# Masking a segment's attention on VectorE with a minimum instead of a TensorE product, with an instruction order made for it

## The chip, the cores and the metric

One core of one Trainium2 chip runs the whole program in one launch. The metric is device time in microseconds (us); lower is better. The kernel before takes 815.55 us, the median of three runs (813.28 to 816.82).

## The reference

Two attentions over the same 2048 rows are mixed by a gate. The change touches only the first, the recurrent one. It goes through 64 segments of 32 rows. Each segment is preceded by 8 memory rows, which are the first 8 output rows of the segment before, so the segments form a chain.

```python
mask = (idx[:, None] < M) | (idx[:, None] >= idx[None, :])   # M = 8, L = 40
for s in range(n_seg):                                       # 64 segments
    h = concatenate([mem, xs]);  q, k, v = h @ Wq, h @ Wk, h @ Wv     # 32 heads of 128
    scores = where(mask, q @ k.T * scale, -1e9)
    o = softmax(scores) @ v @ Wo
    mem = o[:, :M];  outs.append(o[:, M:])
...
return g * a + (1 - g) * b        # b: the second attention, g: the gate
```

A masked score has to count as nothing in the softmax: its exponential must be zero.

## The kernel before, in words

**Parts.** `p_seg` issues one segment. It works in two passes, r = 0 and r = 1, of 16 heads each. The second attention (`p_bproj`, `p_piece`, `p_bout` and others, in units), the projections of the rows that become memory keys (`p_rest`) and the output product of later rows (`p_orest`) do not depend on the chain; they are work that can stand anywhere between.

**One segment.** K, Q and V projections (`wproj`, line 1422) in groups of four products that run side by side on four 32-column strips of the array; each result is copied out of PSUM by `copy` (lines 1000 to 1004, ops `kev`, `qev`, `vev`), which may run on ACT or on DVE. K and Q are transposed on DVE (line 1497, `ktp`, `qtp`). Then for each pass:

- `H` (lines 1504 to 1506): a product of two constant tables, `neg` (a diagonal of -1e9) and `hide` (ones where the mask hides), into 160 of the 224 columns of a PSUM bank. It writes -1e9 at the masked places and 0 elsewhere, and it opens the accumulation (`start=True`).
- `S` (lines 1508 to 1520): 16 score products of 40 columns and 4 of 64, added on top of it.
- `exp` (line 1521): ACT takes the exponential of the 224 columns into `PT` (bf16).
- `U` (line 1536): a product with ones gives the sums; `ln` and `rc` (lines 1540, 1542) on ACT make the reciprocal in f32.
- `nrm` (line 1544) and `nrr` (line 1546): `PT` is multiplied by the reciprocal, in two parts; `nrm` on DVE, `nrr` on DVE or GpSimd.
- `PV`, `PW` (lines 1577, 1586): the products with V; `OTev` copies their result out of PSUM.

The output product follows (`wo`, line 1314), then the transpose of the memory rows (`turn`, `swap`, `hm`, lines 1332 to 1337), which the next segment's projections need.

**Order.** Each of the five engines (PE for TensorE, DVE for VectorE, ACT for ScalarE, POOL for GpSimd, SP for SyncE) runs its instructions in a fixed order. `sequences` unpacks it from the string `ORDER`: for each engine a list of operations, which also says which engine does a copy that may run on either. `schedule` walks these lists; `waits` sets the semaphore waits. The order is so written out beforehand, and nothing is rearranged while the kernel runs.

**Tables.** `p_init` fills `neg` and `hide` (lines 844 to 854) with GpSimd selects at the start; the last of them ends at 37.1 us of the profile, and the first `S` starts at 49.81 us.

Of the kernel before, what the change touches and what calls it, by code (L numbers as in the profile page):

```python
# [8 lines left out]
ALU = mybir.AluOpType  # L9
# [10 lines left out]
    "jybi^^oj}%>U%zo>Jb8OZ<N}L1(=#JDDoS_`pkgh2B0%=U>r|~rbo`cqusO2TW~0a<WCe1=<RUh>xlYGAT@awnt*sMpDAF5er(SIgaCr*VEC!Gp!1GiZ{)5^AJm?7j_+?@1XVC66"  # L20
    "fK}v0dtnjOMt8&ES#TM#+-5CV24f)gF^mT=dd2_h7_tMPi`R}>Q*C+|IKc{F8M+b*CahBw{|@l86F&Jw<gJA$VEhbw5jb2flMdk9=>lxN@wK9KSIXHo05@sWTy_w|B0V@xG|X$k!"
    "5Qc(z>l4d0gO{L*8zySK|+AI=Yc|?i|A>-rv~5b&x$60G`~bF5g;`*UeUgp8#$P~WuO<H3;HrU6qp@?poi!G*1ZFJdo>Z@TR5FXf;4NkN4_;Q_>=tEN6g`@fLb1bpaQZOiBXA>+V"
    "H_fUo0j7tZRV`qWIE%l9QVe4i}WBen=dJJ$-3R$`vD)ECd(}i!6v}wbKMbU|KIybFj0I<yVs21`WWjcz74CIxX<zN6}V_>`=sknfI7Lom-iDQqlY4j3tj35S_u#NIL8@#(|@(^gD"
    "q0MO1`W<fvwgK|q|<WpWYQIAZErNVb+NA!hN)%6Z)m)oCLd#K2<P`G#<>Spirme1+>R!DTrEufjoS2e3LBmW(FSix)!Cv_)X{<k$nW+{BAwE4V<Gi@XNJ6qu-J|I%D~`W1pX(dr6"
    "(Zsdy$M1J#|UcaIjK_A87OP!BGmm~3{MiDW2`b1JS#zG4zYL8z&jn!$w&VgMtAR!PCfvr_vXm#I&D5^58Xr!WX?sD?;Wsu1EGvETU^t@Rm^QJ;WnomV`C2^nywC;mQ$Yfy?Ur|D_"
    "+x^7LIRr4fPb(%|7#Kycye@;J*805BKVblW2D^Y*GHwNd0uQboqwdro;&<wLP(!K-hDODb5;6!@=<%CuNDROMkMxyQ!@7G&;`g2uwoqyYIK2&-U4g}V{#iBP3SzT(=$yDIx0r};d"
    "Nfrr`}5L`NyOOQqQPFs*-F9YE_D=Av!#v~1t^1;Pt@?xMDN{1dK?MP(&QfgfDlfp4L48({ACl!_Z={bdSQl?kBP9gHeF!YDiZ}!fSaJ`F@)>OoG{{7l9QCr;5++xqT}nYJ(f%ef~"
    "c~)u+~#VO0>bU0*1m<2xW-kOk04bH`epzFFYc_HvHD-Ka11iv=>z?H<I=tQX?Qxb~61n`atq8hKl#IxN?r?i*2q4HEG5LAY^gk%flVv+w|Ack1N&eV+-P*$I%~$fqC(V=2F6+_tK"
    "`$8cX!18sAl7csb{#;Jk*=Paxt!Za1~P%cZhXN^zu1U15uA4^8D0gNtMmY~^4ON{QNWB&IM|jnZ6*Xhn-kCz4tQhr7rk=C+VQPuR<@C=B(ynW-%49~@;K9!UNyT@S$JF#tytozt5"
    "C5q%x@h_(LpPy`V@*Acw6w7TY-iq_!{C<tnj^Sg(%r<~diL6o##{=@EL37^jN263L+F9ox%n6xg^Gt&DDu=FUTEBz%LVBu$V;StF#Po6I_Sl#@!P^<e$H^}ZKKyE(N>>^7aeuavs"  # L30
    "k{{#SP{$7ig0u5Y#H#>}Wt<&{zDiRhT?0mtAHBEmPeKPL;WPxrHfu(gCf6ag`T(LL?1@J_fS6ROGaBXcH@L-8_<H^ipOtaX;r-0nFvbWeghvU(DST1;KExcXR$dh9w3HG@%d90<&"
    "ZW<b$c$)3=>3m_l&*Y%8{2^}?JvWB^OX~U;fkSdIUfR$4m;v2B`Bx%y#9>54MH3xB7MT$<H0T`m}T6&coXW6Tz;aqV#X!tpSC9S7t)}gBN}W{riGy>zgB*<TzR7uy-}OUuQyyO)-"
    "siOn$h@AL#ivGJ0EhjT1YoyYvW@MFLY>wp|);&Ib8AT;<D}gmu1TFWeRi2Xv>GoU=hpKt%IM&zyT+LjSMg{%J4pXZF;3H(_mrLFQqV+Mk!eItZb1NzWE}MK`K&_YyvM`A%AvKzYV"
    "6M0H<G6fTl+~AFZw|9zwo$KKdS=2?!i51O%%Fm0IS_mN~K|<SP-X20y3A9NgotFGgo9z#&ED)b^)HyWPWZdZABn)#r-7Kv>_;>|+c47YjIdg`vPoNGMcK=SH8l(t6$@=uwE7Cp>8"
    "J4G5f9fY3Gsdp_1c|2}SxF2o#+IoO!z`7&Dd$OV5rg4fas^_$65>v`>`tO75lLm)1OSd4-&iXHX_h^bH?qYv@SS-tpTj8@=i{0!Fx@dx;B>^y*$&Ibf2aaey?M-8ZvZ+2K906G;w"
    "WHuyZ#$|TBj5~wi3Yz~Vw*NjLKy;YPcpls)v}Wj_Jww``O8;rn?AhSbTfj}M4%p7)QNd<#1yT{P@4!jC%?t&m@28UsI&1?}pF;uNPRSB&F4OJ+^+iK~Symw&j*0|(Ke%>FY#=)BN"
    "0spfp&%?Kz=B6z9)ysf+03461+@^^-o}?i&M^U}c-C+77cFah+fy~TfT9r3H41Qh_k%GH?u0wY8qIIZc3Da0hh!jwt)LdMEzr%qwFd=0Yf$sPLpEI?83~L)1Ja1Ir4Am7O(Z5i7H"
    "sQrz;oYifr9W2n9Nw<l2@YM>RO+vTNqYiL!3<xQL)MTck{vq0&;jvo<Gh^0@8rGT41v2z;L1?*n+3d2;pr7mOweE(dIlIws*&e8XG)n-JF5!io%L><BK7Hv&ktcHjy~mb#d?~jV!"
    "hHj}G5V!QGw)64V9AOABTQzYPI(_@{P9>#MSPW`ymLx8jZ+ez)#j6d+sV=8A(zM$#eqPWZlF9-{?1D%y77{uvWcu*Wk2=1nIHIxroS<Q3gq^AiCitVL6|%S*}&loDNz?@|#Ovrg7"
    "tVs-B{y-BQ})dBi8M82qy(AlnBfoa~TlvstPHxaIbt8p>sJ>DE0b{9e41Ft?THB#-==UG!__3IXK+mmE1QP(Vx{pH-D1WKNm@Fcc2U4-G+QC{ppooCOXH7RU|H$SZ$i`v6)H=-7b"  # L40
    "VYu9TE#oa2e;Z&jsaRW&V{)EovUA||DA8f|LP&=Ln{Y%?&x_<KQD;2W0SBf{m_LaM<h6(5pzs2C2JQ12AqAhbglp-*#);na7n|lyhXr4N4HEHLgWwPD#SSD!HVDR{8{Tu6y*US{T"
    "kwLx);kMarJ>-i{{Z3k#8<PtesK_jfMBE~8$sYcJX(AOU-e^=7McSr$ZHXiS};|I!wb9Pdqj^{>_L5m!wW)1Ls6Lb%H0O&)dMxW-~+*eaNMm3PL2ezgRlUCx~tOTlSM@YAZOAy(+"
    "z^dU-Z??&t7;^!!dagxF)QSuheG>mt@P{{&6k&yP1Anj1uhzysfLXqOsecGwI$Kd#-IvuRHeD@OQnTYhdUyFp@WD)?z{RsFYnxlhNo;lcTNY6C1fJ96$HrHx0|rXq`8t&3>?OYX?"
    "<)v4CH<205=bz9qa^@ie%`w2z&>@rdipAA1>}Y<sNaEnKu|7!KOjkIQ_`aOA`+2z);0%UvJ+8~U&==D!`yqx>Z^gP?-f8^WGLRxBJYiwogJsIWS%SPX(jZ_m)f`L?y(R5c1SxjAF"
    "em3A((TYd)g<DKgO4K}3}ggy+(tB<TAIIyr_ivBEgIMqG7`|tZV8~Nw9D~(7yxX?66;Pox<=z@QIw_#p%1sPj_sQLbL4t`I7jDfJ_Z8&ptNO=pV37awgBQ*N`wG}1~GOjj$hb(@x"
    "$L$wMgZv5_=6w(3`p8ws<7k`RxA?wD+K|&itkvnWA-iuO*&o67enCHF?^!q*%58Z1OtOy7fU|ejn+1Dczju7PY33VEZbgYEJY~*<8jquiU0IN@um83IuqEc;fV9~lbWf`VqK&)Wm"
    "@~|T_g<pj2L%-x!C1<pcE^eLHa#6l!5o)a|8f)IZe0_I*B$SjT>DXlfrGOT6Un`zj+c|WkZq92lVI-X?FktNt3M_87S^#sd~n-hT=Dtxk;_RShz%LNchAa`N5NyA-ii47OK#CbjE"
# [1600 lines left out]
```

## Time and profile before

| | us |
|---|---|
| median of the three runs | 815.55 |
| lowest and highest | 813.28, 816.82 |
| the profiled execution | 813.89 |
| its span, first to last instruction | 811.9 |
| TensorE busy, of the span | 788.2 (97%) |
| VectorE busy | 643.7 (79%) |
| ScalarE busy | 523.1 (64%) |
| GpSimd busy | 257.8 (32%) |

The span is what the rows of the trace cover; 2.0 us of the profiled time lie around it. "PE" in the rows is TensorE's matmul side and "PEld" its weight loads, which overlap it. A matmul's row gives its length, while the next one may start before it ends, so what a matmul costs TensorE is read from the starts, or from the chain of waits, where overlap is taken out. `x4` beside a row counts instructions. The clock that TensorE was granted is 1.00 of full speed over the whole span.

### The profile page before, as it was taken

The page shows a single profiled execution, that of the slowest core. Times are in us where ns is not written, and L with a number is a line of the kernel's source. Part 1 is how long each engine was busy: PE and PEld are TensorE (multiplying, and loading weights), DVE is VectorE, ACT ScalarE, POOL GpSimd, SP SyncE. Part 2 cuts the span into 40 slices and gives each one's busy share as a digit, 9 for nine tenths or more (in the row PEclk, how much of TensorE's full clock was granted, in tenths as well). Part 3 has the DMA queues.
Part 4 walks back from the last instruction along what each step waited for, and adds up shares of the span by engine and source line. Part 5 has one row for each costly group of instructions (what it writes and reads, how often), then busy time and mean ns, then how long its engine had stood idle before and what let it go on. Part 6 is the DMA issues. An engine that isn't in the chain of part 4 may idle for free.

```text
span 811.9 us, 51762 instructions
## 1 busy us (share of the span) xinstructions
PE 788.2 (97%) x23598; PEld 501.2 (62%) x23607; DVE 643.7 (79%) x1681; ACT 523.1 (64%) x1198; POOL 257.8 (32%) x564
## 2 busy tenths in 40 slices
PE   9899999999999999999999999999999999999987
PEld 4456666666666666666666665656766665666655
DVE  4878887788889787787787887786877898787886
ACT  4666656776666656767667666577666656766662
POOL 4542221233223332422422322333323223432440
PEclk9999999999999999999999999999999999999999
DMA  8983202121200111121011111100111010010001
GB/s 327 417 256 63 47 16 45 36 52 27 48 25 21 46 27 40 33 46 34 21 33 48 38 25 42 30 24 20 40 48 31 21 31 21 16 25 22 22 21 37
DMA packets 71696, 45.14 MB, mean 56 GB/s; under 512 B 50046, under 2 KB 69942, under 8 KB 69942
## 3 DMA queue, kind: packets, MB, share of 16 engines
q1 hardware_dynamic: 70422, 40.92, 17.8%
q8 instruction: 185, 3.03, 1.6%
q10 hardware_dynamic: 1056, 0.92, 0.4%
q14 instruction: 33, 0.27, 0.1%
HBM read 30.33 MB, written 8.87 MB: 48 GB/s over the span
## 4 chain that ended last, share of the span: by engine, by line
PE 84%; DVE 8%; DMA 3%; ACT 2%; issue 2%; SPq 1%; POOL 1%; DVEq 0%; POOLq 0%; ACTq 0%
PE pb L1422 46%; PE pb L1314 18%; PE pb L1029 6%; PE pb L1146 3%; PE pb L1187 2%; PE pb L1577 2%; DMA st<-in_gate_w_dram 2%; PE pb L1512 2%; PE pb L1536 1%; PE pb L1031 1%; DVE V_sb L1002 1%; PE pb L1586 1%; DVE st L1002 1%; PE pb L1235 1%; DVE QT_sb L1497 1%
## 5 line engine op out<-in xcount | busy, mean ns | idle before, releaser
L1164 ACT ACTIVATE PTB<-pb 128x640 bf16<-128x640 f32 x240 | 158.5, 705 | 41.0 <-PE pb L1146 29.8
L1002 ACT ACTIVATE st<-pb 128x512 bf16<-128x512 f32 (+2 forms) x232 | 112.9, 499 | 104.3 <-PE pb L1422 76.1
L1422 PE MATMUL pb<-Wv_sb,hT 128*32 128x512 bf16 x2048 | 152.5, 380 | 0.0
L1422 PE MATMUL pb<-Wq_sb,hT 128*32 128x256 bf16 (+1 forms) x3072 | 139.2, 308 | 0.3
L1314 PE MATMUL pb<-Wo_sb,OT_sb 128*32 128x256 bf16 x4096 | 130.8, 273 | 2.2 <-issue 1.8
L1422 PE MATMUL pb<-Wk_sb,hT 128*32 128x512 bf16 x2048 | 131.1, 379 | 1.2 <-issue 0.9
L1314 PEld LDWEIGHTS pb<-Wo_sb,OT_sb 128*32 128x32 bf16 x4096 | 102.3, 96 | 12.6 <-issue 2.3
L1170 POOL TENSOR_SCALAR_AFFINE_SELECT PTB<-PTB 128x512 bf16<-128x512 bf16 x120 | 77.7, 648 | 90.2 <-ACT PTB L1164 82.2
L1422 PEld LDWEIGHTS pb<-Wq_sb,hT 128*32 128x32 bf16 x3072 | 79.7, 97 | 42.4 <-DVE hT L1337 4.4
L1546 POOL TENSOR_TENSOR PT_sb<-PT_sb,rc_sb 128x64 bf16<-128x64 bf16 x81 | 28.9, 356 | 188.9 <-ACT rc_sb L1542 174.9
L1422 PEld LDWEIGHTS pb<-Wk_sb,hT 128*32 128x32 bf16 x2048 | 53.2, 97 | 49.6 <-DVE hT L1337 2.3
L1002 DVE CAST st<-pb 128x512 bf16<-128x512 f32 (+1 forms) x123 | 67.2, 549 | 15.4 <-PE pb L1422 12.7
L1002 ACT ACTIVATE OT_sb<-pb 128x320 bf16<-128x320 f32 (+1 forms) x139 | 57.4, 429 | 32.2 <-PE pb L1586 31.3
L1002 DVE CAST OT_sb<-pb 128x320 bf16<-128x320 f32 (+2 forms) x121 | 56.5, 475 | 18.5 <-PE pb L1586 17.6
L1002 DVE CAST V_sb<-pb 128x512 bf16<-128x512 f32 x90 | 61.5, 684 | 8.8 <-PE pb L1422 7.9
L1497 DVE STREAM_TRANSPOSE QT_sb<-st 128x128 f32<-128x128 f32 (+1 forms) x192 | 61.8, 335 | 8.3 <-ACT st L1002 6.4
L1540 ACT ACTIVATE rc_sb<-pb 128x160 f32<-128x160 f32 x128 | 38.9, 304 | 42.7 <-PE pb L1536 36.2
L1332 DVE STREAM_TRANSPOSE pb<-pb 128x256 f32<-128x256 f32 x63 | 29.3, 465 | 40.7 <-PE pb L1314 40.4
L1521 ACT ACTIVATE PT_sb<-pb 128x224 bf16<-128x224 f32 x128 | 45.5, 356 | 23.0 <-PE pb L1516 19.1
L1422 PEld LDWEIGHTS pb<-Wv_sb,hT 128*32 128x32 bf16 x2048 | 48.0, 97 | 20.0 <-ACT st L1002 0.7
L1497 DVE STREAM_TRANSPOSE KT_sb<-st 128x256 f32<-128x256 f32 x128 | 54.6, 427 | 7.0 <-ACT st L1002 5.5
L1544 DVE TENSOR_TENSOR PT_sb<-PT_sb,rc_sb 128x160 bf16<-128x160 bf16 x128 | 45.2, 353 | 8.9 <-ACT rc_sb L1542 7.3
(200 smaller groups left out, 1449.4 us busy)
## 6 DMA issues: line engine op xcount, KB each, us to landing
Wv_sb<-in_A_Wv_dram SPq DMA_DIRECT2D x4, 1024.0 KB, 11.2
Wk_sb<-in_A_Wk_dram SPq DMA_DIRECT2D x4, 1024.0 KB, 19.3
Wq_sb<-in_A_Wq_dram SPq DMA_DIRECT2D x4, 1024.0 KB, 26.6
Wo_sb<-in_A_Wo_dram SPq DMA_DIRECT2D x4, 1024.0 KB, 22.2
rest_v<-stg SPq DMA_DIRECT2D x112, 32.0 KB
rem_v<-rest_v SPq DMA_DIRECT2D x28, 128.0 KB, 2.5
a_rows<-ao SPq DMA_DIRECT2D x63, 32.0 KB
stg<-a_rows SPq DMA_DIRECT2D x15, 128.0 KB
```

The source lines that it names most:

```text
L1002: self.P.op(("act", "dve"), (lambda a: a.activation(dst, src(), ACT.Copy), lambda d: d.tensor_copy(dst, src())), reads=reads, writes=write ...
L1029: ins = pe.matmul(out[32 * c:32 * c + 32], lhsT[:, 32 * c:32 * c + 32], rhs, start=start, stop=stop, tile_position=(0, 32 * c), **kw)
L1164: P.op("act", (lambda dst=dst, src=src: lambda a: a.activation(dst, src(), ACT.Exp, scale=0.25))(), reads=[pair], writes=["%s%d_%d" % (nam ...
L1170: P.op("gp", (lambda pt=pt, ii=ii: (lambda g: g.affine_select(pt, pt, ([[0, len(ii)]] if len(ii) > 1 else []) + [[1, 128]], ALU.is_ge, 0.0 ...
L1314: ins = pe.matmul(pb[so.b][p0:p0 + 32, 0:256], tok(r, g, l), half(h, d, q), start=(r == 0 and g == 0 and l < 2), stop=(r == 1 and g == 3 a ...
L1332: P.op("dve", lambda d: d.transpose(pb[so.b][:, 256:512], pb[so.b][:, 0:256]), reads=[so], writes=[rt], name="turn%s" % name, cost=0.468, ...
L1422: ins = pe.matmul(self.pb[sl.b][32 * g:32 * g + 32, 0:hi - lo], x[:, c, 0:32], cols, start=(c == 0), stop=(c == C - 1), tile_position=(0, ...
L1497: op("dve", (lambda dst=dst, src=src: lambda d: d.transpose(dst, src))(), reads=["st%d%s" % (i, tag)], writes=["%sT%d%s" % (kind, r, tag)] ...
L1521: op("act", lambda a: a.activation(PT[:, r, :], pb[rb.b][:, 0:224], ACT.Exp, scale=SCALE), reads=[rb], writes=["PT%d" % r, "PT%dr" % r], n ...
L1540: op("act", lambda a: a.activation(rc[:, r, :], pb[rb.b][:, 0:160], ACT.Ln), reads=[rb], writes=[rr], name="ln%d_%d" % (s, r), cost=t_act( ...
L1544: op("dve", lambda d: d.tensor_tensor(mine[r], mine[r], by_head(rc[:, r, :]), ALU.mult), reads=[rp, rr], writes=[rp], name="nrm%d_%d" % (s ...
L1546: op(("dve", "gp"), tuple((lambda e: e.tensor_tensor(rest[r], rest[r], late(rc[:, r, :]), ALU.mult)) for _ in range(2)), reads=[rp + "r", rr],
```

## The change

The product `H` is left out of both passes of every segment. The first score product of each 32-row strip now opens the accumulation. After `exp`, DVE takes the minimum of 160 of the 224 exponentials with a table that holds 0 where the mask hides and 3e38 elsewhere (`cut`). The table is written into `hide` once, at the start: one product of `neg` and `hide` (`keep`), and one DVE instruction that turns it into 0 and 3e38 (`keepev`). `U`, `nrm` and `nrr` of a pass now come after `cut`.

```diff
@@ ORDER
-    "c-nPZ2|yIp8~...
+    "c-nPZ2VfLM7k;...
...
@@ p_init
+        sm = P.slot("F")
+        op("pe", lambda pe, m: self.mm(pe, m, pb[sm.b][:, 0:160], self.neg[:, :], self.hide[:, :], True, True), reads=["neg", "hide"], writes=[sm],
+           name="keep", cost=0.08, prio=-0.98, mode=FLEX)
+        op("dve", lambda d: d.tensor_scalar(self.hide[:, :], pb[sm.b][:, 0:160], -0.5, 3e38, op0=ALU.is_ge, op1=ALU.mult), reads=[sm], writes=["hide"],
+           name="keepev", cost=0.3, prio=-0.98)
@@ p_s
-            def f_hide(pe, m):
-                return self.mm(pe, m, by_head(pb[rb.b][:, 0:224])[:, :, 0:40], self.neg[:, :], self.hide[:, :].rearrange("p (h q) -> p h q", h=4), True, True, skip_group_check=True)
-            op("pe", f_hide, reads=["neg", "hide", "st%d" % i], writes=[rb], name="H%d_%d" % (s, r), cost=0.072, prio=prio, mode=FLEX)
-
...
-                                        start=False, stop=True, tile_position=(0, 32 * g), skip_group_check=True)
+                                        start=(l == 0), stop=True, tile_position=(0, 32 * g), skip_group_check=True)
...
             op("act", lambda a: a.activation(PT[:, r, :], pb[rb.b][:, 0:224], ACT.Exp, scale=SCALE), reads=[rb], writes=["PT%d" % r, "PT%dr" % r],
                name="exp%d_%d" % (s, r), cost=t_act(224), prio=prio)
+            op("dve", lambda d: d.tensor_tensor(by_head(PT[:, r, :])[:, :, 0:40], by_head(PT[:, r, :])[:, :, 0:40], by_head(self.hide[:, :]), ALU.min),
+               reads=["hide"], writes=["PT%d" % r, "PT%dr" % r], name="cut%d_%d" % (s, r), cost=0.3, prio=prio)
```

**The new order, unpacked.** SP's list is the same. The others are rearranged throughout. What can be counted in the two lists:

| | before | after |
|---|---|---|
| `H` / `cut` | 128 / 0 | 0 / 128 |
| `kev` on DVE / on ACT | 42 / 86 | 21 / 107 |
| `vev` on DVE / on ACT | 90 / 38 | 72 / 56 |
| `qev` of 256 columns on DVE / on ACT | 57 / 71 | 36 / 92 |
| `qev` of 512 columns on DVE / on ACT | 24 / 40 | 21 / 43 |
| `OTev` on DVE / on ACT | 121 / 139 | 127 / 133 |
| `par`, `parr` (64-row copies) on DVE / on ACT | 31 / 48 | 39 / 40 |
| `swap` on DVE / on ACT | 93 / 33 | 103 / 23 |
| copies of the second attention's K and Q, DVE / ACT | 17 / 15 | 20 / 12 |
| copies of `p_rest`, DVE / ACT | 46 / 50 | 43 / 53 |
| `nrr` on DVE / on GpSimd | 47 / 81 | 41 / 87 |

Two examples of TensorE's list, from an `S` to its `U`: before, `S31_0`, three groups of `v31_0`, `H31_1`, one more group, `U31_0`; after, `S31_0`, a group of `v31_0`, `q31_1b` (two half-width groups' worth), two more groups, `U31_0`. In DVE's new list the operation just ahead of a `cut` is a Q transpose 31 times, a K transpose 22 times, a V copy 21 times and a `nrm` 17 times; just behind it stands a `nrm` 30 times, a Q transpose 28 times, a V copy 18 times and a K transpose 10 times. `keep` stands 36 operations ahead of the first `S` on TensorE.

More of the change, by code (lines that the diff above doesn't have):

```diff
@@ L20 @@
[L20 to L47, printed above, removed]
@@ L76 @@
[L76 to L79 removed]
+    "c-nPZ2VfLM7k;yQm)&b=1f&NDgx-tvDumudT2Pwwj{F296zK>8p-77;9YI7CLI^!-q=q68>7b|-NlY%>C3m+o|IA+5axrk1yV*ByUin@ds9f>|hr{`NKn8ea#0$9j3%O4m2G1%EJ"
@@ new lines @@
+    "iSV9S^Djzt}S5J+V2Hu&)W}QSZn>+Y<tndaXUJ(_C@%7>c_SOaAcm}n{)nB7&PB<_zsl)1I!EN58As1eq6fR<uokLUp%()LlE;V`Aeo0f0GaJ{gcuS0Lp#UZtTf-(sF+JY<gVBv;"
+    ")^KrMm$5m&Nl#va_lQ0OmJM;p96zj)6VIbtKC(`Eo&vt%I&T8tpo}Ye=iDP^Vc2cpgC^7~?Y@7Jmr<6@Y-t*iy=9{k-hyE-5W9*A>t9No{;JH?&!XHO9QHTGq(qDQ<AU?ZM+e0tf"
+    "-`PpShzC=lQS#7n$o);wtS>!G$__B6^AVgDdI9I4TA^AG^hOTFm=G`ZLW7D!trxx;dc)k%+h4WiQmP#ZsV!||9#jGLGAyJC=M>t;iU=Y`x?rT?s%ZSgS5qwl#PGkMRO0M8U~itsv"
+    "eki;XSV2^-Y2+t7=uni`;;Y{X2g=2Yu_W<^XNIYX1VntlG)$Q#3BeckLL!;#|^PWO`W6+!$aI0o7FH-}xr@`$uypF8?<oA;B*VReS0+djWz8YNy5g8+1gpFUCTa4;teOS(Eg+oK!"
@@ new lines @@
+    "u$n%dr|`Ys2Mz(WqHK}Hxp1!4BV=3cRxl5T%`kddNrmePNFE7EcahPJY%>?og)o<g2l#Zp8}|QjK(YUXyO+M)2#=^v5rw%?|3XAI2!@N$_)?p5&0!rSn5OVNHU^-|J*o?(mW&Wm2"
+    "+u1%DkoH-k8WD+l;xh1ofXdC{0uujfD~kc0u)i0V|oEqax9O^8sPo;wcN0RQY=#RYFLfF-Gbk#Vm3Qp>>mhsI?ce2k{F3!f<6GtN;fb%jgr8QuW+JP@m$x|QC9oWZb$n7^=_eZ{>"
+    "Ic_>HE|z6agjjbB(q<=2sr>#&SXd2YUd9Dty<JH^D!}=1EouJDyp~$<g<?bT@37sYtnQ!G@QgNk*!^Pyn!Uj*tj2hcc#T3d+HZ*y^P+=Iwl66x{Y5<1P6cV5(Y`ENJtvkqo8##b1"
+    "_z@E>am?8sa7;cBDZv3FykjdE@htfEc^laJ}0G9Wg%mDA!{y=!2ud<Rxhk_3hGLVz=ktOq1sa9eVzP+|LfGS0OhxFHrk8?3Os32^bF^sWp{tL8bu>T!hUSiq7WqLwpCMrWuG^bAL"
@@ new lines @@
+    "LEAe-s3Ygt+FmJ4)cJ!Fd085usb4xZSGlM`gO8rc8;ykEMfvXU1$*d1>1yUu!O@pKRK}yOQ+yL*uPtQs)V9ZfYzXtt!WGxwpP|Yk$ZViCnB43*vmi%d3WW41b9Vctk|7%8jFJbw;"
+    "WLVY#(I4s{N+GoWsRf*AcLvNCsafgCUnrc9!yEG@Xf%tOsnBLOSRs$Xqg4j1-FL$cU%r^D$U7eP45oSKNWcVgEJIT&UA;@-gmItS6ygWQ)iC}YnQ4K`2w`R6fhQL3i?BD|4u@gvr"
+    "uPGhr<(l!uokm}&6xWNj>nsXY#6=!^Z(gl<5bvcpQZ3!PG2zvD+=X&ChI0plf8-BJOYyYsN?=pW5~YOWCB9PU!ll?6Rp5x;G}<{7yw6ODW73m;riW)J%z(keFg*ga?FDoF4)kdkt"
+    "KiqbV#4O@WRL1JOwcisQ5-F%W4H%N6|bjtbnOc%Ukk4n+1D91}mJ;MV_x23DCpOd-hVVlk42C%mQ5%F4b4e1b87(&59K|!Imcq)8;OO4HK4u28TBwrhzv*01IU9T0LM8r2Y?8cu_"
@@ new lines @@
+    "-4hrZ3M{<Qmd$uQ^RN-U4GO@o`$RyS1m&8zGD4d4gK81+2N9+3++{#0`ZSkHB(@c&}E5+tK&x=oLp9I#Q`S)nPMYjf2f^?~GAHBKt^g16)vDJzyl;aER6Z2S?vQN-);V9k1JKr;;"
+    "yL9Pm6cOaU@=IQR&YSKakJt=K^D=#t4P!KYpLZE_#U4@#SET|#Esg8E|8TvA3n$EOiv}t2E(LWI44Jl(DWY(wnNN-j9ra1*Vz@GU}6(LGEsmz5TX1B!ei{Cvuv1(s1Il{O0Gk-PI"
+    "x_&4nTYj$1Tvhy+t$Gr`hD?Q07)7+@x0*CZxQutswuSmM1N@PoaGnbA)zHQZ6^UJ*uSNiDo18Qbs!!PPK%p#lv>Q_|o*I=pv{^=k%PyDk>QCHIY0T!=Z&X3D4+iWX0BWWb0jp*M7"
+    "rkhl;wDSU{q((~w~iU*3{J`HC7zaoKWT1K^ck`Q;C79+QtJ#!_Im^?;#OF?$PM3&RQP3X{w582dFAs04mOWrfEyE|N>4LSb%3j{9W*cd{OQUy^YCxjg?4V(H&)?B^V66w$Ex8=7i"
@@ new lines @@
+    "X_^tK;AoNcwqy(&V-(O~Gw&8ydr}ZZ*)J)z4&q`XU~=!<_K#2$#pfN*|T2dhf$3BY!;(wtWvN{!`_e*6TYkcQ{V#06bDS)`2Cz(8h=YoS|11uYRV?F!|HR3cqmJ@vd2<7PjOrPn7"
+    "d8u+~E(oFkeAisfl>V66%Gs|oLWY@)A7FA870^_;bhwU8yJIQ+{_wYrSwI)dS7)GO!#2H%d8EU`yFxkIBo4?1ELfzj97j$pJKKRvh+qYtOA?2b{xkx&Kaz^GJ=R&n@TE1E2;-nW?"
+    "Ts6N*;Q*_pGKlF&<#hlne<!GJ_F=wGp=@U54@hh|d`?miv_=M+{K>XI}_BBf(TL?u!8$pDpynW%gv=z_JEeQ^%%?us}N(-Q4cnm^e@@mP$y*(lV+ac&1x-UM=UcxB~Ub<R?zvjaN"
+    "I~)C4=@Ha@RGv9Qrg586x`Gu@Uz`<@gZyMCdIEY870cQ?PJrx^lnlYhgZ-}2^AhlSC$0P7w!qBY5G7T5qOeczh``zrUnp;sY%W27s*l0rh~TglqHqb+>6FdxE)5Q&*~3!@cS#A2<"
@@ new lines @@
+    "YiIW0boMdHgBJiqKWRb<q2RHSI_2fSRJOKOye=3O81lB!s{g48!Epc!YO)~HJV(4Xq>Y~Zi$$@Y^#aZhzh*#>xyYq{FR?n&#J;uQ<9q2NTGj)mQGkTKN9D}dI{MPu}=~7KGWtOiA"
+    "p9>wZbJXhAxGMg4t&c#@!49@tUd?1;)$~4xVexp>~+ua<o0qDBLw4&RaKnMIGrzePpA1WHAxcuL6q)2h^cLB5X~me0Lm!Jf&)Ri4mT}3w_>UyOz_Yxh(u!M&jjdbjjWD4#L@Oq&`"
+    "Q&a#0Cz*f@$34u7%dcI~hacF9`U#nfIGo8pC0G4EEB2bwACyfQEw!=fs9t{fhI*E%fJL7~8h`d1k&sBPx2vgNmX9r=uxbrA9`p2dq0SkAS(d1iIM7*+0=A@sZ9$sZyw71#x8Y+F@"
+    "1-gkcF6l>q5+_+CaYG4dN?&90<L;TLwQfYAd-S0fxhr=^cmO!FnWhz715t!_Eg_DxeX1p2VZT65bnUfiF_!OQcc@h3wV;V3SU0IV56(aehmX)^BVrYC3Y6<w+E{Yru9f-e<iOAtg"
@@ L80 @@
+    "J|ox^o^gFnYKX<8oSi@<ct8x0gO0_eq|W+x&Y}apZ*?Mm5;o4uaeg&26xfnh7{;4Q1)s-6c7>Jm6ZP$RW%~(=4RhFqzVsp-5{EVGw=@=Ky;T#N&^>A7X8O%CqddSl@OyF%hyKOH{"
+    "Kx3VfL9*as%)2UF~?u*o~OPC>cFRu)+>eOCsem+j}lO05M3Yp#cWUlE(q#dM}UYZXYl2KX~}>-03d%S3Qn1IjGm@ab6%$ZXR_bKqa69X~5zfrh%losn>+2S12zC0wqErLK?UDViD"
+    "<Xll~8w$TxZ"
 )
```

72 lines of the change are left out of this document (36 added, 36 removed).

## Prediction

> **What bounds the kernel now.** I read the page's busy times and its chain of waits, then the chain piece by piece in one stretch, then the waits of TensorE's weight loads, then the durations of the instructions that the change touches.
>
> ```profile
> PE 788.2 (97%) x23598; PEld 501.2 (62%) x23607; DVE 643.7 (79%) x1681; ACT 523.1 (64%) x1198; POOL 257.8 (32%) x564
> PE 84%; DVE 8%; DMA 3%; ACT 2%; issue 2%; SPq 1%; POOL 1%; DVEq 0%; POOLq 0%; ACTq 0%
> 52.00:782.00 730.00, 717.13 (x22098) 462.25 (x22090) 589.32 (x1540) 482.98 (x1112) 227.87 (x486) 1.00 0.15 34
> 782.00:812.00 30.00, 23.82 (x727) 15.48 (x716) 21.84 (x57) 10.15 (x29) 4.83 (x11) 1.00 0.12 35
> ```
>
> The last two rows give a stretch, its length, and the busy time of PE, PEld, DVE, ACT and POOL. From 52 to 782 us TensorE is busy 717 of 730 us at the full granted clock; only at the end, where little independent work is left, does it fall to 79%. The chain that sets the end is TensorE for 84%, DVE for 8% and ACT for 2%; its DMA and SP parts belong to the loads at the start. So work taken from TensorE counts almost whole, and work given to DVE counts only where DVE sets the pace.
>
> ```profile
> 399.87 0.22 PE pb L1422 x4
> 400.09 0.10 PE pb L1536 x8
> ...
> 409.83 0.07 PE pb L1029 x4
> 409.90 1.30 PE pb L1422 x32
> ...
> 412.00 0.07 PE pb L1029 x4
> 412.07 0.22 PE pb L1422 x4
> ...
> 423.13 0.07 PE pb L1029 x4
> ```
>
> These are pieces of the chain: start, length, what. L1029 with four products is `H` here. Its product lasts 0.23 us by its own row, but the next projection starts 0.07 us after it: 0.07 us is what one `H` takes from TensorE.
>
> **The change, part by part.** The sum is made against the profiled execution, 813.9 us (span 811.9 and 2.0 around it); the median of the runs is 1.7 higher.
>
> *`H` goes.* 128 products at 0.07 us are 9.0 us. TensorE has 84 of the 96 parts of the chain that lie behind the start (84 + 8 + 2 and some issue and POOL), so 0.88 of it: **-7.9 us**. Ends: 9.0 if all of it counts, 7.5 at the plain 84%. `keep` gives back one 0.07 at the start.
>
> ```profile
> 36.90 0.22 POOL L853 TENSOR_SCALAR_AFFINE_SELECT hide_sb<-hide_sb 32x32 bf16<-32x32 bf16 x1
> 49.81 0.27 PE L1512 MATMUL pb<-QT_sb,KT_sb 128*32 128x40 bf16 x16
> ```
>
> It needs the last table select, which ends at 37.1 us, and stands 36 operations ahead of the first `S` at 49.8; the startup work between hides it and `keepev`. Without that cover it would cost their lengths and handovers once, under 1 us.
>
> *`cut` comes, on DVE.* The trace shows no product or minimum of two 16-bit tensors there. The nearest rows:
>
> ```profile
> L1544 DVE TENSOR_TENSOR PT_sb<-PT_sb,rc_sb x128: 261/326/792, 52.1 to 804.6; 128x160 bf16<-128x160 bf16 x128
> L1546 DVE TENSOR_TENSOR PT_sb<-PT_sb,rc_sb x47: 206/219/453, 68.9 to 803.6; 128x64 bf16<-128x64 bf16 x47
> L1544 DVE TENSOR_TENSOR PT_sb<-PT_sb,rc_sb 128x160 bf16<-128x160 bf16 x128 | 45.2, 353 | 8.9 <-ACT rc_sb L1542 7.3
> L1280 DVE TENSOR_SCALAR t_sb<-stg,g_sb 128x512 f32<-128x512 bf16 x15 | 7.7, 515 | 1.1 <-POOL orow L1244 1.0
> L1092 DVE TENSOR_SCALAR etmp<-stg 128x512 bf16<-128x512 bf16 x8 | 2.2, 271 | 0.1
> ```
>
> The first two give least, median and longest ns. `nrm` has the same 160 elements, but one factor in f32: median 0.33, mean 0.35. 64 elements take 0.22. The last two rows show that on this engine an instruction with 16-bit data throughout can take half the time of one with f32. So `cut` lies between 0.22 and 0.35 us; I take **0.27**, the middle of 0.22 and 0.33.
>
> The Trainium skill (VectorE: DVE Perf Modes, "The perf-mode tier table (the rule you actually need)") lets a two-tensor instruction run two elements a cycle when all is 16-bit in SBUF, and one with f32. With the formula under its section on the errata, (N + 151) / 0.96 ns, I estimate 324 ns at one a cycle, which `nrm`'s median of 326 agrees with, and 241 ns for `cut`. By 0.24 the sum below would be about 1 us lower.
>
> DVE gets 128 x 0.27 = 34.6 us. The new order takes copies from it:
>
> ```profile
> L1002 DVE CAST V_sb<-pb 128x512 bf16<-128x512 f32 x90 | 61.5, 684 | 8.8 <-PE pb L1422 7.9
> L1002 DVE CAST st<-pb 128x512 bf16<-128x512 f32 x66 | 44.5, 675 | 9.6 <-PE pb L1422 8.5 <-PE pb L1029 0.3
> L1002 DVE CAST st<-pb 128x256 bf16<-128x256 f32 x57 | 23.0, 404 | 5.8 <-PE pb L1422 4.2 <-PE pb L1029 0.6
> L1002 ACT ACTIVATE st<-pb 128x512 bf16<-128x512 f32 x126 | 75.2, 598 | 69.2 <-PE pb L1422 65.8 <-PE pb L1029 2.4
> L1002 ACT ACTIVATE V_sb<-pb 128x512 bf16<-128x512 f32 x38 | 22.5, 593 | 0.6 <-PE pb L1422 0.2
> L1002 ACT ACTIVATE st<-pb 128x256 bf16<-128x256 f32 x71 | 27.0, 383 | 15.6 <-PE pb L1422 10.4 <-DVE ao L1345 4.2 <-PE pb L1029 0.6
> ```
>
> 21 `kev` and 3 whole `qev` at 0.675, 18 `vev` at 0.684 and 21 half `qev` at 0.404 are 37 us. The small copies that come back to DVE I estimate at 7 us. Net -30, so DVE goes to about 648 us, 0.7% more. Its 8% of the chain is 65 us: **+0.4 us**. ACT gets 24 x 0.598 + 18 x 0.593 + 21 x 0.383 = 33 us, less about 7: 5% more on its 2% of the chain (16 us): **+0.8 us**. POOL gets 6 more `nrr`, hidden at 32% busy.
>
> *`cut` stands between `exp` and `U`.* It is a new wait of DVE on ACT. Behind it in DVE's queue stand `nrm`, Q transposes (the other pass's `S` waits for them) and V copies (`PV` waits for them). What waits for it is `U`, then `ln`, `rc`, `nrm`, `PV`.
>
> ```profile
> 401.15 0.36 ACT L1521 ACTIVATE PT_sb<-pb 128x224 bf16<-128x224 f32 x1 [0.21 <-PE pb L1516]
> 401.55 0.28 PEld L1536 LDWEIGHTS pb<-PT_sb,ones_sb 128*32 128x32 bf16 x8
> 401.73 0.28 PE L1536 MATMUL pb<-PT_sb,ones_sb 128*32 128x160 bf16 x8
> PEld pb L1536 <- ACT PT_sb L1521: 9.3, 40, 0.4
> ```
>
> `exp` ends at 401.51, `U`'s weights load 0.04 us later, the product follows 0.18 us after that. One more link adds 0.27 + 0.04 = 0.31 us. I priced TensorE's work between each `S` and its `U` in both lists by the chain's pieces (0.22 a projection group, 0.10 a `U`, 0.07 an `H`): 0.89 us on average before, 1.18 after. The new order covers 0.29 of the 0.31. The 0.02 left, at the 40 of 128 that waited already: **+0.8 us**. With `cut` at 0.35 it is 0.10 x 40 = 4.0; with 0.22, nothing.
>
> *The end.* After 782 us two segments run with little to cover a longer chain; there `H` was worth nothing extra. Each pays 0.31 - 0.07: **+0.5 us**.
>
> Sum: 813.9 - 7.9 + 0.4 + 0.8 + 0.8 + 0.5 = 808.5; on the median's level **810 us**. With `cut` at 0.22 and all of `H` counted: -9.0, DVE nothing, ACT +0.8, `U` nothing, end +0.4, so 806.1, or 808 on the median. With 0.35: `H` -7.5, DVE +1.5, ACT +0.8, `U` +4.0, end +0.6, so 813.3, or 815. Beyond the terms, the lists are rearranged throughout, which can move any other wait: TensorE is idle for 12.9 us of the 730 and 6.2 of the last 30, and I estimate that the new order may save or lose up to 5 of these 19. That puts the low end at 803.
>
> **The rivals.**
>
> *The saving is taken back ahead of `S`.* TensorE's work between a pass's last K or Q projection and its `S`, priced in the same way, shrinks from 1.80 to 1.62 us (r = 0) and from 1.48 to 1.23 (r = 1), 0.22 on average.
>
> ```profile
> PEld pb L1512 <- DVE QT_sb L1497: 3.7, 13, 0.5
> PEld pb L1512 <- DVE KT_sb L1497: 2.5, 9, 0.5
> PEld pb L1577 <- DVE PT_sb L1544: 5.1, 16, 0.8
> ```
>
> 22 of 128 `S` already waited for transposes; at 0.22 each they give back 4.8 us: 813.3, or 815 on the median, no change. Against it: 24 fewer copies of 512 columns stand in DVE's queue ahead of the transposes, and ACT does such a copy 0.08 us faster.
>
> *Slower: `cut` starts late.* DVE is 79% busy with instructions of 0.4 to 0.7 us, runs them in order, and the one ahead of `cut` is a V copy of 0.68 us 21 times and a transpose 53 times. A `cut` that starts late delays `U` directly, since its spare time is used up. Each 0.1 us of mean lateness costs 12.8 us; from 0.04 on the gain is gone (5.4 / 128). At 0.1 the time is 808.5 + 12.8 = 821, or **823** on the median. For it: `PV`'s weight loads waited 16 times for `nrm` (the last row above), so DVE can be late on this path. Against it: that is 16 of 128, and the order puts `cut` mostly behind transposes that are needed before `S` and so are done before `exp` can start.
>
> *`cut` and GpSimd get in each other's way.* If a `cut` had to wait for a GpSimd instruction in flight, which is so 32% of the time, half of a mean 257.8 / 564 = 0.46 us, the cost is 128 x 0.07 = 9.4 us: 818, or 820 on the median. `nrm`, which also reads two tensors from SBUF, speaks against it: its mean is only 0.03 above its median. The Trainium skill (SBUF - State Buffer, "Who interferes with whom") says that a DVE instruction with two SBUF inputs contends with a GpSimd one that reads SBUF, and that the one that starts first blocks the other; `nrm`'s longest of 792 ns would fit that, the 0.03 says that it is rare.
>
> **How the numbers follow.** A measurement of this kernel can tell about 0.5% from no change: faster is below 811.5, slower above 819.6. Chances: the forecast 0.52, its own range 806 to 815 (0.43 below 811.5, 0.09 within); the same with other waits saved too, below 806, 0.09; the saving taken back 0.13 (0.03 faster, 0.10 same); GpSimd 0.05 (0.03 same, 0.02 slower); `cut` late 0.21. That gives faster 0.55, same 0.22, slower 0.23. The range runs from 803 to 823, so that the late-`cut` case at 0.1 us is in it and its worse half is out.
>
> **What would show it.** Right: no more four-product rows of `hide` and `neg` but one; TensorE's busy time about 9 us lower and still 97% of the span; a DVE row of 128 minima near 0.27 us; DVE busy near 648 and ACT near 549; waits of `U`'s weight loads moved from `exp` to DVE and near 9 us in all. Wrong: those waits at 20 us or more, or `cut` starting more than 0.1 us after `exp` on average (late `cut`); waits of `S` for the transposes above 11 us (taken back); minima with a mean far above their median (GpSimd); a TensorE share under 96% with DVE above 10% of the chain.

## The result and the profile after

The changed kernel takes **819.04 us** (median of 20 runs, 817.01 to 822.4) beside 815.2 us for the kernel before in the same job (median of 20, 813.28 to 818.75): a ratio of 1.0044, with a 95% interval of 1.0032 to 1.0056. It is slower by 3.8 us, where 5.5 us less had been forecast. The profiled execution took 822.4 us, 3.4 above its median, with a span of 820.7; that of the kernel before took 813.89, 1.3 under its median. So the two traces lie 8.8 us apart in their spans, where the medians lie 3.8 apart: the traces show where time goes, and overstate how much.

The page of the changed kernel, its busy times and its chain by engine:

```profile
PE 791.4 (96%) x23102; PEld 493.0 (60%) x23102; DVE 651.7 (79%) x1765; ACT 546.8 (67%) x1237; POOL 258.9 (32%) x570
PE 79%; DVE 7%; DMA 5%; ACT 3%; SPq 3%; issue 2%; POOL 1%; DVEq 0%; POOLq 0%
```

DVE and ACT came out as summed (648 and 549 had been forecast). TensorE did not: 496 matmul rows less, and yet its busy time rose by 3.2 us, so this number does not follow the work alone. That it holds waits too is a reading; no row here separates them.

The minimum on `PT_sb` (shortest, median and longest ns), and the weight loads that waited (what they waited for: us in all, times, longest):

```profile
L1524 DVE TENSOR_TENSOR PT_sb<-PT_sb,hide_sb x128: 194/242/614, 50.2 to 811.8; 128x160 bf16<-128x160 bf16 x128
```

```profile
PEld pb L1539 <- DVE PT_sb L1524: 17.1, 59, 0.9
PEld pb L1580 <- DVE PT_sb L1547: 9.4, 24, 0.8
...
PEld pb L1513 <- DVE QT_sb L1502: 8.3, 37, 0.4
PEld pb L1513 <- DVE KT_sb L1502: 8.0, 24, 0.9
```

The minimum (L1524) lasts 0.242 us in the median. `U` (L1539) now waits for it 59 times and 17.1 us, where it waited 40 times and 9.3 us for `exp`; `S` (L1513) waits 16.3 us for its transposes, where it waited 6.2; `PV` (L1580) waits 9.4, where it waited 5.1. Every wait of the chain S, U, PV is longer. That says that the chain is late, not what makes it late, nor where.

For the place, the memory transpose `turn` (L1332 before, L1337 after) serves as a clock: there is one in each of segments 0 to 62. First and last start in the two kernels:

```profile
L1332 DVE STREAM_TRANSPOSE pb<-pb x63: 450/465/466, 57.0 to 793.0; 128x256 f32<-128x256 f32 x63
```

```profile
L1337 DVE STREAM_TRANSPOSE pb<-pb x63: 432/465/466, 58.6 to 802.3; 128x256 f32<-128x256 f32 x63
```

736.0 us before, 743.7 after. Cut at the `turn` of segments 0, 6, 24, 48 and 62, the busy times by stretch (stretch, its length, then PE, PEld, DVE, ACT, POOL) of the kernel before and of the changed one:

```profile
57.00:134.90 77.90, 76.68 (x2348) 47.73 (x2340) 64.46 (x165) 48.24 (x110) 21.52 (x47) 1.00 0.23 44
134.90:346.70 211.80, 208.87 (x6469) 136.20 (x6465) 172.16 (x455) 141.62 (x328) 65.07 (x139) 1.00 0.15 36
346.70:637.30 290.60, 283.37 (x8665) 184.59 (x8664) 227.28 (x604) 193.03 (x446) 88.07 (x186) 1.00 0.14 34
637.30:793.00 155.70, 153.03 (x4788) 97.03 (x4783) 129.75 (x332) 102.37 (x238) 55.12 (x119) 1.00 0.08 22
```

```profile
58.60:134.80 76.20, 75.92 (x2328) 47.04 (x2324) 57.54 (x158) 57.02 (x129) 22.69 (x49) 1.00 0.25 50
134.80:351.30 216.50, 209.40 (x6334) 134.05 (x6326) 174.36 (x477) 148.47 (x342) 64.97 (x141) 1.00 0.14 35
351.30:639.30 288.00, 281.81 (x8465) 180.11 (x8461) 232.90 (x637) 200.35 (x455) 90.69 (x192) 1.00 0.15 34
639.30:802.30 163.00, 155.46 (x4686) 96.29 (x4681) 138.03 (x371) 101.50 (x230) 52.98 (x114) 1.00 0.08 21
```

Segments 1 to 6 and 25 to 48 got shorter (by 1.7 and 2.6 us), segments 7 to 24 longer (4.7), and the fourteen segments 49 to 62 longer by **7.3 us**, 0.52 each. The granted clock is 1.00 throughout. The experiments take the change apart by kind first, and then by stretch.

### The profile page after: what moved, and what is told of

It is laid out like the page before. It is cut to its first block, busy times and chain, and to the rows that moved or that the text cites. A ratio compares the mean times of both kernels' runs of the same rounds, so it can differ in the third digit from the quotient of the medians.

```text
span 820.7 us, 50892 instructions
## 1 busy us (share of the span) xinstructions
PE 791.4 (96%) x23102; PEld 493.0 (60%) x23102; DVE 651.7 (79%) x1765; ACT 546.8 (67%) x1237; POOL 258.9 (32%) x570
## 4 chain that ended last, share of the span: by engine, by line
PE 79%; DVE 7%; DMA 5%; ACT 3%; SPq 3%; issue 2%; POOL 1%; DVEq 0%; POOLq 0%
PE pb L1427 43%; PE pb L1319 17%; PE pb L1034 5%; DMA Wq_sb<-in_A_Wq_dram 4%; PE pb L1151 3%; PE pb L1580 2%; PE pb L1192 2%; PE pb L1513 2%; PE pb L1539 2%; PE pb L1036 1%; SPq L899 1%; DVE PT_sb L1547 1%; SPq L1396 1%; PE pb L1589 1%; DVE V_sb L1007 1%
## 5 line engine op out<-in xcount | busy, mean ns | idle before, releaser
L1007 ACT ACTIVATE st<-pb 128x512 bf16<-128x512 f32 (+2 forms) x274 | 133.3, 500 | 89.9 <-PE pb L1427 73.4
L1427 PE MATMUL pb<-Wv_sb,hT 128*32 128x512 bf16 x2048 | 154.9, 379 | 0.0
L1427 PE MATMUL pb<-Wq_sb,hT 128*32 128x256 bf16 (+1 forms) x3072 | 142.5, 308 | 0.5 <-DVE hT L1342 0.4
L1549 POOL TENSOR_TENSOR PT_sb<-PT_sb,rc_sb 128x64 bf16<-128x64 bf16 x87 | 33.2, 382 | 194.1 <-ACT rc_sb L1545 187.6
L1427 PEld LDWEIGHTS pb<-Wk_sb,hT 128*32 128x32 bf16 x2048 | 55.0, 97 | 50.5 <-DVE hT L1342 2.8
L1007 ACT ACTIVATE OT_sb<-pb 128x320 bf16<-128x320 f32 (+1 forms) x133 | 55.5, 428 | 35.8 <-PE pb L1589 34.8
L1007 DVE CAST OT_sb<-pb 128x320 bf16<-128x320 f32 (+2 forms) x127 | 59.7, 476 | 22.1 <-PE pb L1589 21.1
L1427 PEld LDWEIGHTS pb<-Wv_sb,hT 128*32 128x32 bf16 x2048 | 50.5, 97 | 20.2 <-ACT PT_sb L1522 0.3
L1337 DVE STREAM_TRANSPOSE pb<-pb 128x256 f32<-128x256 f32 x63 | 29.2, 464 | 38.2 <-PE pb L1319 37.3
L1007 DVE CAST st<-pb 128x256 bf16<-128x256 f32 (+1 forms) x78 | 43.1, 553 | 12.8 <-PE pb L1427 11.7
L1007 DVE CAST V_sb<-pb 128x512 bf16<-128x512 f32 x72 | 49.1, 682 | 4.2 <-PE pb L1427 3.1
```

Of the source, the lines that this page charges most:

```text
L1007: self.P.op(("act", "dve"), (lambda a: a.activation(dst, src(), ACT.Copy), lambda d: d.tensor_copy(dst, src())), reads=reads, writes=write ...
L1337: P.op("dve", lambda d: d.transpose(pb[so.b][:, 256:512], pb[so.b][:, 0:256]), reads=[so], writes=[rt], name="turn%s" % name, cost=0.468, ...
L1427: ins = pe.matmul(self.pb[sl.b][32 * g:32 * g + 32, 0:hi - lo], x[:, c, 0:32], cols, start=(c == 0), stop=(c == C - 1), tile_position=(0, ...
L1549: op(("dve", "gp"), tuple((lambda e: e.tensor_tensor(rest[r], rest[r], late(rc[:, r, :]), ALU.mult)) for _ in range(2)), reads=[rp + "r", rr],
```

## The experiments

The "lists" of a kernel are its written orders for the five engines. An edit of the lists is shown by the operations that it moves. Medians of different jobs can be set side by side, since the kernel before came to between 815.1 and 815.5 us in all of them.

### The parts alone

*The product out, the order of before* (nothing masks the scores):

```diff
-            op("pe", f_hide, reads=["neg", "hide", "st%d" % i], writes=[rb], name="H%d_%d" % (s, r), cost=0.072, prio=prio, mode=FLEX)
...
-                                        start=False, stop=True, tile_position=(0, 32 * g), skip_group_check=True)
+                                        start=(l == 0), stop=True, tile_position=(0, 32 * g), skip_group_check=True)
```

> Order of before, H left out and nothing in its place (no masking at all, so the probabilities of masked places stay in). This prices H alone. Theory 1 (H takes 0.07 us of TensorE's path, and the change lost that gain elsewhere): 815.2 - 8 = 807, at least 805. Theory 2 (H lay in time that TensorE would have waited anyway, so there was nothing to gain): 813 to 815, no change.

Measured: **811.66**, ratio 0.9956 (0.9944 to 0.9968). The product is worth 3.8 us (815.5 - 811.66; about 2.6 to 4.6 by the interval), not 7.9, between what the two theories have.

*The same with the minimum*, put into DVE's list of before where `exp` had ended in the trace; the rest of the order stays:

```diff
+            op("dve", lambda d: d.tensor_tensor(by_head(PT[:, r, :])[:, :, 0:40], by_head(PT[:, r, :])[:, :, 0:40], by_head(self.hide[:, :]), ALU.min),
+               reads=["hide"], writes=["PT%d" % r, "PT%dr" % r], name="cut%d_%d" % (s, r), cost=0.3, prio=prio)
```

> Order of before, H out, cut in, each cut put into DVE's old list at the place where its exp ended in the trace of before; nothing else moved. Theory 1a (cut costs time because it stands between exp and U and the order must make room): well over the changed kernel's 819, about 825 to 830, since 0.28 us more are added to a path that had about 0.2 to spare. Theory 3 (the new order as a whole is the worse one, cut itself is cheap): below 819, about 810 to 815.

Measured: **839.27**, 1.0289 (1.0275 to 1.0302). `U`'s waits in its list of waits:

```profile
PEld pb L1538 <- DVE PT_sb L1523: 66.0, 118, 1.3
```

Without room the minimum costs 27.6 us, 0.22 of its 0.24 for each of the 128, and 118 of 128 `U` wait. So the order had to be remade; the question is what the new one costs.

*The changed kernel without its minimum* (nothing masks; lists of after):

```diff
-               reads=["hide"], writes=["PT%d" % r, "PT%dr" % r], name="cut%d_%d" % (s, r), cost=0.3, prio=prio)
```

> The changed kernel's order with cut left out (no masking at all). Theory 1a (cut on the path from exp to U took the gain back): 819 falls to about 807, and the waits of U's weight loads from 17 us to under 5. Theory 3 (the new order is the worse one): stays at 815 to 818.

Measured: **816.62**, 1.0017 (1.0003 to 1.0031). With room made, the minimum costs 819.04 - 816.62 = 2.4 us, give or take 1.5 by the two intervals. But the new order without either is 816.62 - 811.66 = **5.0 us** slower than the old order without either.

*The computation of before in the order of after*, each product directly ahead of its `S`:

> The computation of before in the changed kernel's order: cut out, H back, each H directly ahead of its S. Theory 3 (the order is worse by itself): clearly over 815.2, about 820 to 826. Theory 1a: about 814 to 816, as H costs its 8 to 9 us on top of the kernel without both.

Measured: **821.79**, 1.0075 (1.0061 to 1.0089), 6.3 us over the kernel before: the order loses with the product too, and the product, placed so, costs 821.79 - 816.62 = 5.2 us there. The three parts, -3.8 + 5.0 + 2.4, lead from the kernel before to the changed one step by step, so they add up by construction: what is measured is the parts, and their sum is no test of them.

### Where the order loses: lists joined at a segment

Two lists can be joined: the one up to the moment when a segment's `turn` starts, then all that has not begun, in the order of the other. First at segment 52, from where on each traced kernel in the new order fell behind:

```text
lists of after up to the turn of segment 51,
then lists of before for all that has not begun
```

> Neither the mask product nor the minimum (the scores are not masked at all, so the output is not the reference's): lists of the changed kernel up to the end of segment 51, lists of the kernel before from segment 52 on. Known: the lists of before without the product 811.7, the changed lists without the minimum 816.6. Theory A (the changed lists cost nothing until segment 51, and lose about 0.5 us in each of the last twelve segments, where the chain S, exponential, U, reciprocal, PV, output product sets the pace and not TensorE's work): 811 to 812.5. Theory B (the changed lists lose a little in every segment, through the shorter filling ahead of S): 12 of 64 segments are given back, 815.5 to 816.

Measured: **817.99**, 1.0035 (1.0019 to 1.0051). A miss for A, and above what B allows.

> Whole computation. Segments 0 to 51 as in the changed kernel (no product, minimum), segments 52 to 63 as in the kernel before (product, no minimum), with the lists of each. Known: before 815.5, after 819.0. Theory A (the loss of the change lies in the last twelve segments alone): 814 to 815.5, so the kernel before or a little better. Theory B (the loss is spread over all segments): after's 819.0 less 12/64 of 3.8 us, 818 to 818.5.

Measured: **821.23**, 1.0066 (1.0046 to 1.0086). A miss for both. In the traces of these two the `turn`s fall 3.5 us behind between segments 51 and 54 and run within 1.5 us of before's pace from there to 62: the cost sits at the join. There the two lists have begun sets that differ by 20 operations: a projection of the second attention, a load of its weights, eight small transfers and others that the new lists had put off fall due at once. That these operations, falling due at once, are what costs the time is a guess, and which of them was not tried.

> Whole computation. The other way round: segments 0 to 51 as in the kernel before (product), segments 52 to 63 as in the changed kernel (minimum). Theory A: the whole loss of the last twelve segments without the small gain ahead of them, 820.5 to 822. Theory B: 12/64 of the loss, 816 to 816.5.

Measured: **821.04**, 1.0071 (1.0044 to 1.0098), as A has it, though with a join of the same kind, so not clean.

> Whole computation. Minimum in segments 0 to 6 and 30 to 48, where the changed kernel gained on the kernel before in the two traces (about 3.1 and 3.4 us); product in segments 7 to 29 and 49 to 63; lists of the one or the other by segment. Theory A (a segment's time depends on its own lists, and gains of stretches add up): 809 to 811. Theory B (the gains of the stretches are paid back where the lists are joined, or were a loss put off): 815 to 818.

Measured: **813.85**, 0.9978 (0.9965 to 0.9992): faster than both kernels, but short of what A has. In its trace the first stretch puts it 1.5 us ahead of the kernel before at the `turn` of segment 6, not 3; at that of segment 30 it is 3.3 us behind, though segments 7 to 29 have the lists of before.

Then at segment 49, where the sets differ by no more than eight operations:

> No masking at all (neither product nor minimum). Lists of the changed kernel up to the end of segment 48, lists of the kernel before from 49 on; at this joint the two lists have begun almost the same operations (8 of 6662 differ, against 20 at the joint of the first splice). Known: lists of before 811.7, changed lists 816.6; in their traces the two differ by 0.9 us at segment 48 and by 6.3 at segment 62. Theory A (the changed lists lose in segments 49 to 62 alone; the first splice missed through its joint): 812 to 813.5. Theory B (the loss is spread): 815 to 816. Theory C (any join of lists costs 3 us or more): 815.5 or more.

Measured: **812.61**, 0.9966 (0.9951 to 0.9980). A. Of the order's 5.0 us, 816.62 - 812.61 = 4.0 lie in segments 49 and later; the 1.0 us ahead of them is within the noise.

> Whole computation. Segments 0 to 48 as in the changed kernel (minimum), 49 to 63 as in the kernel before (product), lists of each. In the two traces the changed kernel is 1.1 us ahead at segment 48 and 6.2 behind at segment 62. Theory A: 814 to 815. Theory B: 818 to 818.5. Theory C: 817.5 or more.

Measured: **813.41**, 0.9978 (0.9962 to 0.9994), below the range of A, and with the mixed kernel the fastest full computation of this study.

> Whole computation. Segments 0 to 48 as in the kernel before (product), 49 to 63 as in the changed kernel (minimum). Theory A: the 7.3 us that the changed kernel loses in these segments, 821.5 to 823.5, slower than the whole change. Theory B: 15/64 of the loss, 816.4.

Measured: **823.29**, 1.0093 (1.0073 to 1.0114). A. The change in the last segments alone is slower by 7.9 us, about twice the loss of the whole change. The last stretch of four kernels (segments 49 to 62; before 155.70, after 163.00): the old order without a mask, the new order without a mask, the minimum up to 48, the minimum from 49.

```profile
634.50:791.30 156.80, 153.12 (x4676) 95.32 (x4672) 129.80 (x332) 102.55 (x239) 55.16 (x119) 1.00 0.08 22
```

```profile
635.10:797.30 162.20, 154.71 (x4682) 97.95 (x4678) 132.03 (x342) 102.08 (x231) 54.01 (x116) 1.00 0.08 21
```

```profile
635.10:792.10 157.00, 153.92 (x4788) 98.82 (x4783) 130.00 (x331) 101.93 (x237) 55.06 (x120) 1.00 0.09 22
```

```profile
641.10:804.10 163.00, 154.54 (x4666) 95.36 (x4670) 137.91 (x371) 101.57 (x230) 52.83 (x113) 1.00 0.08 21
```

In these traces the stretch goes by its own lists: 156 to 157 us in the order of before, 162 to 163 in that of after, with or without product and minimum. The matmuls in it are as many in both orders without a mask (4676 and 4682 rows), so the new order does not lose there by leaving more work to these segments.

> Whole computation. Minimum in segments 25 to 48 alone, where the changed kernel gained 2.6 us on the kernel before (after losing 4.6 in segments 7 to 24); product and the lists of before in all others. Theory A (each stretch keeps its own gain or loss): 812.5 to 813.5. Theory B: 24/64 of the loss, 816.8. Theory C: 817 or more.

Measured: **816.74**, 1.0016 (1.0001 to 1.0031). A miss for A, and what B has (816.8): the 2.6 us that segments 25 to 48 had gained in the traces did not come alone.

### What it is in the last segments: a later `U`

Mean starts over segments 52 to 61, in us since the `turn` of the segment before, worked out from the trace records by operation:

```
            before   old order,   new order,   after
                     no mask      no mask
S, r = 0     4.71      4.71         4.72        4.66
U, r = 0     5.68      5.69         5.99        5.98
U, r = 1     7.16      7.14         7.62        7.72
PV, r = 1    8.88      8.92         9.38        9.44
first wo     8.95      8.96         9.51        9.55
turn        11.09     11.14        11.64       11.68
```

`S` of r = 0 stands where it stood. `U` stands 0.3 and 0.5 later, since the order puts more filling ahead of it, and all that follows is later by the same 0.5, to the next `turn`. In segments 20 to 47 a like delay of `U` (0.25) is gone by `turn` (11.90 in both orders without a mask). To test it, `U` is moved behind one more piece of filling in the old order, no mask, first in the last segments, then in the others; TensorE's work is the same:

```diff
-v56_0_1 U56_0 v56_0_2 v56_0_3
+v56_0_1 v56_0_2 U56_0 v56_0_3
```

> No masking at all. Lists of before without the product (811.7), and in segments 49 to 62 alone 18 of 28 `U` stand behind one more piece of filling (0.22 us each, 3.9 us in all), the total work unchanged. Theory A (there the chain of a segment sets the pace, and a later U is paid in full): 815 to 816. Theory B (the filling only changes places, TensorE's total is the same): 811.5 to 812.5.

Measured: **815.57**, 0.9998 (0.9985 to 1.0011). A: 3.9 us for 3.9 us moved, or 2 to 5 by the intervals of the two runs. Its last stretch took 160.1 us, where the old order without a mask took 156.8:

```profile
634.40:794.50 160.10, 153.13 (x4676) 95.72 (x4672) 130.24 (x332) 102.31 (x239) 55.82 (x119) 1.00 0.08 22
```

> No masking at all. The same in segments 25 to 48: 39 of 48 `U` stand behind one more piece (8.5 us in all). Theory A (in these segments TensorE's work sets the pace, and a later U is mostly hidden): 811.7 to 814. Theory C (a later U is paid in full anywhere): 820.

Measured: **817.06**, 1.0019 (1.0008 to 1.0030): 5.4 us for 8.5 us moved (about 4 to 6.5 by the intervals), between A and C. Its own stretch, and that of the old order without a mask and without the move:

```profile
348.30:637.40 289.10, 281.25 (x8476) 177.27 (x8472) 227.07 (x604) 191.13 (x446) 88.13 (x185) 1.00 0.14 34
```

```profile
347.90:634.50 286.60, 280.32 (x8477) 178.21 (x8471) 227.33 (x604) 192.04 (x446) 87.45 (x185) 1.00 0.14 35
```

2.5 us lie in that stretch, 0.3 for each us moved. But the trace is of the fastest of twelve executions (814.78 us, 2.3 under the median), and its whole span is only 2.9 us longer than that of the kernel without the move (812.6 and 809.7). The median says 5.4 us, 0.6 for each us moved, and no trace shows where the rest of it lies. The trace records, averaged over each stretch, agree with the trace's figure: in segments 49 to 62 `U` of r = 0 starts 0.24 us later and the next `turn` 0.24 us later; in segments 25 to 48 it starts 0.25 us later and the `turn` 0.11. So part of a later `U` is hidden ahead of segment 49, and no hiding shows behind it; how much is hidden stays open, between 0.4 and 0.7 of what was moved.

### What a product is worth

> Kernel before, the mask product left out in segments 49 to 62 alone (their scores are not masked), 28 products or 1.7 us of TensorE's work less. Theory A (the chain sets the pace there): 815 to 816, no gain. Theory B (every product is worth the same, 3.9/128 us): 814.6; by its full duration 813.7.

Measured: **817.63**, 1.0024 (1.0009 to 1.0040): 2 us slower for 28 products less, so no gain, as A has it, and above its range.

> Kernel before, the mask product left out in segments 25 to 48 alone (their scores are not masked), 48 products or 3.0 us of work less. Theory A (TensorE's work sets the pace there, and nearly the whole gain is made there): 811.7 to 812.7. Theory B (every product is worth the same): 814.

Measured: **816.65**, 1.0013 (1.0001 to 1.0024). A miss for A: no gain here either.

```diff
             op("pe", f_hide, reads=["neg", "hide", "st%d" % i], writes=[rb], name="H%d_%d" % (s, r), cost=0.072, prio=prio, mode=FLEX)
+            if 25 <= s < 49:
...
+                op("pe", f_hide, reads=["neg", "hide", "st%d" % i], writes=[rb], name="HH%d_%d" % (s, r), cost=0.072, prio=prio, mode=FLEX)
```

> Whole computation. Kernel before, in segments 25 to 48 each mask product made twice in a row (the second writes the same values): 48 products or 3.4 us of TensorE's work more. Theory A (TensorE's work sets the pace there): 818 to 819.5, and the stretch from segment 24 to 48 longer by 2.5 to 4. Theory D (the product fills time in which TensorE waits anyway, so that neither more nor fewer of them count, and what moved is a scatter of 1 to 2 us that any edit brings): 814 to 817.

Measured: **816.38**, 1.0004 (0.9987 to 1.0022). D: 3.4 us of work more cannot be told from none, and the interval ends at 1.8 us. In the one trace kept (an execution 2.6 us above the median) the stretch took 292.4 us from `turn` to `turn`, where the kernel before took 290.6: 1.8 more, under the 2.5 that A needs.

> Whole computation. The same in segments 49 to 62: 28 products or 2.0 us of work more. Theory A (the chain sets the pace there and the product waits with S for the keys and queries, so it is hidden in part): 815.5 to 816.5. Theory B (the product stands in the chain ahead of S and is paid each time): 817.5. Theory D: 814 to 817.

Measured: **818.53**, 1.0041 (1.0020 to 1.0062). Above A, and above the 817.5 of B: 3.4 us for 2.0 us of work, with an interval from 1.6 to 5.1 us that holds the 2.0.

Neither taking products out of a stretch nor adding them in segments 25 to 48 moves the time by their work; adding them in the last segments does. The 3.8 us come only with all 128 left out, and no run places them: segments 0 to 24 alone were not tried.

## Why the prediction was wrong, point by point

- **The step that failed first: where the end begins.** The prediction took TensorE for the bound up to 782 us, from a busy share of 98%, and charged a longer chain only to the two segments behind that: +0.5 us. A longer chain is paid from segment 49 on, at about 637 us. There the room made for the minimum is not cover but delay: fourteen segments at 0.52 us, 7.3 us in the traces, 4.0 us between the medians of the two kernels without masks. Where the loss lies is shown by the joined lists; that the later `U` makes it rests on the table of starts and on the run that moved `U` in the old order. The reverse, the new order with `U` moved forward, was not run.
- **The same fact in the sum's words**: "the new order covers 0.29 of the 0.31" is right, and the cover was counted as free. It is so only where the filling that is put ahead of `U` is missed nowhere else.
- **The rearranged lists** were given no term, but a bound of 5 us to either side. They cost +5.0, at the very end of that bound. This term and `H` make the miss: 5.0 for the order and 4.1 for `H` are 9.1 us, and the time came out 9.3 us away from the forecast (-5.5 forecast, +3.8 measured).
- **`H` was mis-sized**: -7.9 forecast, -3.8 measured. The 84% of the chain is a share of names, not of a price. The old order without products has its waits elsewhere; `S` there waits 9.1 + 6.0 us for its transposes, against 6.2:

```profile
PEld pb L1505 <- DVE QT_sb L1494: 9.1, 29, 0.7
...
PEld pb L1505 <- DVE KT_sb L1494: 6.0, 19, 0.6
```

- **`cut` came out right, in part by luck.** The terms for DVE, ACT, `U` and the end sum to 2.5; with room made it cost 2.4. But the ACT term and the copies in DVE's term belong to the rearranged lists, which the kernel without the minimum has too, and the term for the end rested on the step that failed. The length was right: 0.27 forecast, 0.242 in the median and 0.265 in the mean (33.9 us of DVE for 128).

```profile
L1524 DVE TENSOR_TENSOR PT_sb<-PT_sb,hide_sb 128x160 bf16<-128x160 bf16 x128 | 33.9, 265 | 10.3 <-ACT PT_sb L1522 8.0
```

The estimate of 0.241 us that the prediction worked out from the Trainium skill (VectorE: DVE Perf Modes, "The perf-mode tier table (the rule you actually need)", with the formula of its section on the errata) agrees with this median.

- **The rivals.** *Taken back ahead of `S`*: the sign that had been named, over 11 us of waits of `S` for transposes, came (16.3), but the cause was not the shorter filling ahead of `S` as such: with the new order up to segment 48 the time is 812.6, 1.0 over the old order, and the old order without products has 15.1 us of these waits too. *`cut` late*: in the records it starts 0.09 us after `exp` ends in the mean, 0.03 in the median, and `U`'s waits of 17.1 us stayed under the 20 that had been named; taking the minimum out gives back 2.4 us, so this is not the loss, though 0.09 us of lateness at the prediction's 12.8 us for each 0.1 would have made 11.5. *GpSimd*: mean and median of the minimum differ by 0.023 us, 2.9 us of DVE time in all. No rival had the mechanism that decided.
- **The range** (803 to 823) held the time. Faster had 0.55. The measured 1.0044 lies just inside the 0.5% that had been called no change, and its interval reaches over it; no effect at all (1.0) is far outside that interval.
